# Data-carrying holds on GpSimd, meant to make weight loads and chunk loads take turns

## The chip, the cores and the metric

One NeuronCore of a Trainium2 chip runs the whole program; the other cores are idle. The metric is the device time of one execution in microseconds (us), lower is better. Most executions of the kernel before lie within 1.5% of its fastest; a run that is over 1.5% above the fastest of its kernel is called slow and left out of the ratios. A ratio is the mean time of one kernel's fast runs over the mean of the other's fast runs of the same rounds on the same chip, so it is not quite the ratio of the medians that are quoted beside it. Intervals are 95%.

The engines are TensorE (PE, its weight loads PEld), VectorE (DVE), ScalarE (ACT), GpSimd (POOL) and SyncE (SP). SyncE issues the loads of the inputs and the stores. GpSimd issues the loads of the weights, which are cast to bf16 on the way (6.3 MB of fp32 in HBM; its queue moved 3.15 MB by the page of before).

## The reference

A gated linear attention with a state per head, then an MLP with a squared ReLU, on 3072 tokens (4 batches of 768):

```python
for t in range(S):                       # B, H, S, D = 4, 8, 768, 48
    state = alpha[:, :, t, :, None] * state + einsum('bhd,bhe->bhde', k[:, :, t], v[:, :, t])
    y[:, :, t] = einsum('bhd,bhde->bhe', q[:, :, t], state)
x = y.transpose(0, 2, 1, 3).reshape(B * S, H * D)      # 3072 x 384
h = x @ w_in                                           # w_in 384 x 2048
r = maximum(h, 0); out = (r * r) @ w_out               # w_out 2048 x 384
```

## The kernel before

The tokens come in 24 chunks of 128. A chunk needs four loads of 192 KB: `at` (alpha), `qt`, `kt`, `vt`. Its chain opens on ScalarE with the logarithm of `at`, then TensorE sums the logarithms with a triangular matrix (the matmul that the profile shows as L_s, utri_b), ScalarE takes exponentials, VectorE scales q and k, TensorE does the attention. The MLP runs in groups of chunks: the first group is chunks 0 to 3 with 512 tokens, then single chunks 4 and 5, then pairs.

The kernel doesn't write its instructions in the order in which it emits them. It first fills a `Plan` with operations, each with an engine, an estimated duration and what it depends on. A small list scheduler runs the plan and sorts the operations by planned start. Only then does each `emit`. Calls wrapped in `pin` keep that order on their engine; the compiler may still move those that aren't. The loads of SyncE are not wrapped; in the changed kernel `at` of chunk 4, first of its chunk in the source, is issued eighth, and in e2, which wraps those of chunks 4 and 5, first:

```python
def pin(ins):
    tc.keep_in_program_order(ins)
...
def load_w(dst, src, ready):             # a weight part, on GpSimd
    def e_issue():
        pin(nc.gpsimd.dma_start(out=dst, in_=src))
    issue = add("POOL", W_ISSUE, e_issue, w_gate[0], prio=-3.0, lat=0.0)
    ready.append([add("DMA", WLD, lambda: None, issue, lat=2.0)])
...
def add_gate(d):                         # weights wait for qt of chunk 3
    def e_hold():
        pin(nc.gpsimd.tensor_copy(hold, d["qt"][:, 0, 0:1]))
    w_gate.append(add("POOL", 0.1, e_hold, d["ld_qt"], prio=-6.0))
...
def add_loads(s):                        # the four loads of a chunk, on SyncE
    ...
        def ld(nm=nm, src=src):
            d[nm] = loads.tile([P, H, D], FP32, name=nm)
            nc.sync.dma_start(out=d[nm], in_=src[b, c])
        prev = C[s - LB]["use_" + nm] if s >= LB else None
        d["ld_" + nm] = add("DMA", LD, ld, prev, lat=2.0, at=0.6)
...
DMA_ORDER = [0, 1, 2, 3, "i", "i", "i", "i", "o", "o", "o", 4, "o", 5]
```

`DMA_ORDER` is what the plan believes of the transfers: chunks 0 to 3, four parts of w_in ("i"), w_out in four parts ("o") with chunk 4 before the last. On the chip SyncE and GpSimd issue on their own, so the list does not order the transfers of one against those of the other: `at` of chunk 4, behind seven weight parts in the list, was issued at 15.18 us, the first weight part at 17.52. It does decide when the plan thinks that a chunk is there, and with it where TensorE's fixed order takes the chunk up.

Of the kernel before, what the change touches and what calls it, by code (L numbers as in the profile page):

```python
# [8 lines left out]
FP32 = mybir.dt.float32  # L9
# [101 lines left out]
def kernel(  # L111
# [10 lines left out]
    nc = tc.nc  # L122
    B, H, S, D = q.shape
    HD = H * D
    P = 128
# [6 lines left out]
    FT = d_ff // P  # L132
# [11 lines left out]
    loads = ctx.enter_context(tc.tile_pool(name="loads", bufs=LB))  # L144
# [26 lines left out]
    w_out_b = consts.tile([P, FT, d_model], BF16)  # L171
# [12 lines left out]
    def pin(ins):  # L184
        tc.keep_in_program_order(ins)
# [20 lines left out]
    LD = 1.02  # L206
# [3 lines left out]
    def add(eng, dur, emit, *deps, **kw):  # L210
        return plan.add(Op(eng, dur, emit, deps, **kw))


    w_in_ready, w_out_ready = [], []
    NWP = 4

    W_ISSUE = 0.8
    W_GATE = 3
    hold = consts.tile([P, 1], FP32)

    def load_w(dst, src, ready):
# [5 lines left out]
    def load_w_in(i):  # L227
        w = d_ff // NWP
        sl = slice(i * w, (i + 1) * w)
        load_w(w_in_b[:, :, sl], w_in_r[:, :, sl], w_in_ready)  # L230

    def load_w_out(i):
        w = FT // NWP
        sl = slice(i * w, (i + 1) * w)
        load_w(w_out_b[:, sl, :], w_out_r[:, sl, :], w_out_ready)

    w_gate = []

    def add_gate(d):
        def e_hold():  # L240
            pin(nc.gpsimd.tensor_copy(hold, d["qt"][:, 0, 0:1]))
        w_gate.append(add("POOL", 0.1, e_hold, d["ld_qt"], prio=-6.0))

    C = [dict() for _ in range(NT)]
    state = {}

    def add_loads(s):
        d = C[s]
        b, c = divmod(s, NCH)
        for nm, src in srcs:  # L250
            def ld(nm=nm, src=src):
                d[nm] = loads.tile([P, H, D], FP32, name=nm)
                nc.sync.dma_start(out=d[nm], in_=src[b, c])
            prev = C[s - LB]["use_" + nm] if s >= LB else None
            d["ld_" + nm] = add("DMA", LD, ld, prev, lat=2.0, at=0.6)

    def add_chunk(s):
        d = C[s]
# [219 lines left out]
        add("OUT", 0.55, e_out, ev, at=0.0).late = OUT_LATE  # L478
        return op

    DMA_ORDER = [0, 1, 2, 3, "i", "i", "i", "i", "o", "o", "o", 4, "o", 5]
    for d in DMA_ORDER + [s for s in range(NT) if s not in DMA_ORDER]:
        if d == "i":
            load_w_in(len(w_in_ready))
        elif d == "o":
            load_w_out(len(w_out_ready))
        else:
            add_loads(d)
            add_chunk(d)
            if d == W_GATE:  # L490
                add_gate(C[d])
    b1 = b2 = None
    FIRST_PARTS = [[0, 1], [2, 3]]
    for g in range(NG):
# [74 lines left out]
```

## Time and profile before

| kernel before | |
|---|---|
| time, median of 3 runs | 200.13 us (200.09 to 201.14) |
| span of the profiled execution | 199.3 us |
| TensorE busy | 93% |
| TensorE's one long wait after 24 us | 1.82 us, for part 1 of w_out |
| TensorE idle from 45 to 80 us | 4.4 us |

The page, TensorE's timeline and SyncE's queue are shown in the prediction below. What is not shown there is GpSimd's timeline. Its columns are start, duration, engine and line, operation, output and input, count, and in brackets the idle time before it with what ended it:

```profile
17.40 0.19 POOL L241 COPY hold<-qt 128x1 f32<-128x1 f32 x1 [2.55 <-DMA qt<-in_q_dram]
17.52 2.43 POOL L223 DMA_DIRECT2D w_in_b<-in_moe_w_in_dram  x3
...
21.18 3.01 POOL L223 DMA_DIRECT2D w_out_b<-in_moe_w_out_dram  x4
```

One copy of one column, the gate, keeps all eight weight parts back until qt of chunk 3 has landed, at 17.34 us. Then they are issued together, from 17.52 to 24.19. From there the weights of GpSimd and chunks 4 and 5 of SyncE share the DMA engines: from 30 to 35 us each of the two queues moved 956 packets, 0.73 MB of weights and 0.18 MB of chunks.

The matmul that opens chunk 4 stands late in TensorE's order, after 44 of the 64 w_out matmuls of the first group:

```profile
44.65 0.32 PE L188 MATMUL bank<-L_s,utri_b 128*128 128x384 bf16 x1
```

### The profile page before, as it was taken

Reading aid. Unit: us, or ns where it says so; the run is one execution under the profiler, and the core shown is the slowest. Engines: PE = TensorE matmul, PEld = TensorE weight load, DVE = VectorE, ACT = ScalarE, POOL = GpSimd, SP = SyncE. Lnnn points to the kernel's source line nnn. Section 1 sums busy time; section 2 is a strip of 40 time slices with the busy share of each in tenths; the row PEclk is TensorE's granted clock in tenths of the full one; section 3 lists DMA queues with packets and bytes.
Section 4 is the critical chain, followed back from the end, with each engine's and each line's share of the span. In section 5 each row is a group of like instructions: output and inputs, shape, how many; then the busy total and the mean of one; then the engine's idle time right before and its main releaser. Section 6 shows DMA issues by size and latency. Waiting matters only on the chain.

```text
span 199.3 us, 5184 instructions
## 1 busy us (share of the span) xinstructions
PE 184.8 (93%) x1921; PEld 130.6 (66%) x1924; DVE 138.4 (69%) x359; ACT 132.7 (67%) x380; POOL 23.3 (12%) x46
## 2 busy tenths in 40 slices
PE   7887799699588999999999999999999999999993
PEld 2445444356476787778777777777777777777761
DVE  0599646206999998698888888888888778754300
ACT  3366279317598898668779778867977786656510
POOL 5125801002111111101101101110110000000000
PEclk9999999999999999999999999999999999999999
DMA  6998999999999899989997975231001101100122
GB/s 128 216 194 163 185 191 185 185 187 215 195 216 238 184 190 219 207 174 232 204 233 156 230 171 118 44 79 44 31 9 44 39 3 39 43 26 16 42 81 79
DMA packets 107034, 27.08 MB, mean 136 GB/s; under 512 B 100352, under 2 KB 107008, under 8 KB 107008
## 3 DMA queue, kind: packets, MB, share of 16 engines
q1 hardware_dynamic: 103296, 23.60, 56.4%
q0 software_dynamic: 3712, 3.15, 9.8%
q8 instruction: 15, 0.25, 0.5%
q14 instruction: 11, 0.09, 0.1%
HBM read 25.17 MB, written 4.72 MB: 150 GB/s over the span
## 4 chain that ended last, share of the span: by engine, by line
PE 64%; DVE 2%; DMA 2%; ACT 1%; issue 0%; ACTq 0%; DVEq 0%
PE bank L188 56%; PE bank L191 5%; PE sc L188 2%; DMA out_dram<-ob 2%; PE st L188 1%; DVE gT L441 1%; ACT r L435 1%; DVE sm L342 1%; DVE qkT L326 0%; DVE xT_big L397 0%; ACT ob L472 0%; DVE st L363 0%; ACT L_s L267 0%; ACTq L435 0%; ACTq L472 0%
## 5 line engine op out<-in xcount | busy, mean ns | idle before, releaser
L435 ACT ACTIVATE r<-bank 128x256 bf16<-128x256 f32 (+2 forms) x192 | 68.8, 385 | 23.3 <-PE bank L188 20.2
L188 PE MATMUL bank<-xT_big,w_in_b 128*128 128x256 bf16 (+2 forms) x576 | 79.4, 272 | 1.5 <-ACT r L435 1.0
L188 PE MATMUL bank<-w_out_b,gT 128*128 128x384 bf16 x384 | 74.3, 326 | 1.8 <-DMA w_out_b<-in_moe_w_out_dram 1.8
L441 DVE TENSOR_TENSOR gT<-r 128x256 bf16<-128x256 bf16 (+2 forms) x192 | 55.1, 305 | 19.1 <-ACT r L435 17.6
L188 PEld LDWEIGHTS <-w_in_b 128*128 128x128 bf16 x576 | 48.6, 97 | 16.2 <-issue 2.8
L188 PEld LDWEIGHTS <-gT 128*128 128x128 bf16 x384 | 36.6, 98 | 19.4 <-issue 2.3
L342 DVE TENSOR_TENSOR sm<-sc,utri_b 128x512 bf16<-128x512 f32 x48 | 32.6, 685 | 3.9 <-PE sc L188 3.8
L273 POOL CAST vb<-vt 128x384 bf16<-128x384 f32 x24 | 14.3, 594 | 121.6 <-PE bank L188 68.3
L309 DVE TENSOR_TENSOR qA_s<-qt,A 128x384 bf16<-128x384 f32 x24 | 13.8, 576 | 17.7 <-ACT A L290 17.6
L472 ACT COPY ob<-bank 128x384 f32<-128x384 f32 x23 | 11.0, 480 | 17.7 <-PE bank L188 16.7
L326 DVE COPY qkT<-bank 128x1024 bf16<-128x1024 bf16 x24 | 16.5, 689 | 6.4 <-PE bank L191 6.4
L188 PEld LDWEIGHTS <-qkT 64*128 64x128 bf16 (+1 forms) x272 | 10.8, 95 | 10.4 <-DVE gT L441 4.1
L290 ACT ACTIVATE A<-bank 128x384 bf16<-128x384 f32 x24 | 11.8, 491 | 8.7 <-PE bank L188 8.6
L368 ACT CAST sb<-st 128x384 bf16<-128x384 f32 x20 | 9.6, 479 | 7.5 <-DVE st L363 7.4
L267 ACT ACTIVATE L_s<-at 128x384 bf16<-128x384 f32 x24 | 12.6, 524 | 2.2 <-DMA at<-in_alpha_dram 2.2
L312 DVE TENSOR_TENSOR kI_s<-kt,Ainv 128x384 bf16<-128x384 f32 x24 | 13.8, 576 | 0.2 <-ACT Ainv L294 0.2
L386 ACT CAST xn<-bank 128x384 bf16<-128x384 f32 x24 | 11.5, 478 | 3.1 <-PE bank L188 3.1
L188 PE MATMUL bank<-warm 128*128 128x512 bf16 x33 | 11.2, 477 | 1.3 <-DVE ae_s L181 1.3
L294 ACT ACTIVATE Ainv<-bank 128x384 bf16<-128x384 f32 x24 | 11.8, 492 | 0.0
L188 PE MATMUL sc<-qkT 64*128 64x128 bf16 x192 | 9.5, 218 | 2.1 <-DVE qkT L326 2.0
L363 DVE TENSOR_TENSOR st<-st,ae_s 128x384 f32<-128x384 f32 x20 | 11.1, 556 | 0.0
L191 PE MATMUL bank<-ident_bf,qA_s 128*128 128x128 bf16 x96 | 9.3, 219 | 1.1 <-DVE qA_s L309 0.6
(38 smaller groups left out, 125.9 us busy)
## 6 DMA issues: line engine op xcount, KB each, us to landing
at<-in_alpha_dram SPq DMA_DIRECT2D x24, 192.0 KB, 3.7
qt<-in_q_dram SPq DMA_DIRECT2D x24, 192.0 KB, 3.9
kt<-in_k_dram SPq DMA_DIRECT2D x24, 192.0 KB, 3.8
vt<-in_v_dram SPq DMA_DIRECT2D x24, 192.0 KB, 3.8
out_dram<-ob SPq DMA_DIRECT2D x24, 192.0 KB, 2.3
w_in_b<-in_moe_w_in_dram POOLq DMA_DIRECT2D x4, 384.0 KB, 9.0
w_out_b<-in_moe_w_out_dram POOLq DMA_DIRECT2D x4, 384.0 KB, 16.9
```

What stands on the lines that cost most here:

```text
L188: pin(nc.tensor.matmul(*a, **kw))
L191: pin(nc.tensor.transpose(*a))
L267: pin(nc.scalar.activation(L[:, :, 0:D], d["at"], AF.Ln))
L273: pin(nc.gpsimd.tensor_copy(d["vb"], d["vt"]))
L290: pin(nc.scalar.activation(d["A"], d["pm"][:, 0:HD].rearrange("p (h d) -> p h d", h=H), AF.Exp))
L294: pin(nc.scalar.activation(d["Ai"], d["pm"][:, 0:HD].rearrange("p (h d) -> p h d", h=H), AF.Exp, scale=-1.0))
L309: pin(nc.vector.tensor_mul(qA[:, :, 0:D], d["qt"], d["A"]))
L312: pin(nc.vector.tensor_mul(kI[:, :, 0:D], d["kt"], d["Ai"]))
L326: pin(nc.vector.tensor_copy(d["qkT"], d["pT"]))
L342: pin(nc.vector.tensor_mul(d["sm"][:, hh], d["sc"][:, hh], utri_b.to_broadcast([P, NP, P])))
L435: pin(nc.scalar.activation(box["r"][:, 0:n], box["ph"][:, 0:n], AF.Relu))
L441: pin(nc.vector.tensor_mul(gT[g][:, f, 0:n], box["r"][:, 0:n], box["r"][:, 0:n]))
```

## The change

The intent is that transfers take turns: w_in and the first part of w_out run alone, then chunk 4 is let go, then the second half of w_out, then chunk 5. A load is held by letting GpSimd write one column of its destination tile from a weight part. The load overwrites that column, so it has to wait for the copy, and the copy waits for the weight part (in the changed kernel part 0 landed at 32.73 us, the copy ran from 32.78 to 32.97, the load was issued at 35.51; in e2 the copy ran at 31.10 and the load was issued at 31.32). A second gate holds parts 2 and 3 of w_out behind qt of chunk 4. The core of the diff:

```diff
-    def add_gate(d):
+    def hold_w(d):
         def e_hold():
             pin(nc.gpsimd.tensor_copy(hold, d["qt"][:, 0, 0:1]))
-        w_gate.append(add("POOL", 0.1, e_hold, d["ld_qt"], prio=-6.0))
+        w_gate[:] = [add("POOL", 0.1, e_hold, d["ld_qt"], prio=-6.0)]
+
+    def hold_x(d, i):
+        j = i * FT // NWP
+
+        def e_hold():
+            d["at"] = loads.tile([P, H, D], FP32, name="at")
+            pin(nc.gpsimd.tensor_copy(d["at"][:, 0, 0:1], w_out_b[:, j, 0:1]))
+        d["go"] = add("POOL", 0.1, e_hold, w_out_ready[i][0], prio=-6.0)
 ... (in add_loads)
-                d[nm] = loads.tile([P, H, D], FP32, name=nm)
+                if nm not in d:
+                    d[nm] = loads.tile([P, H, D], FP32, name=nm)
                 nc.sync.dma_start(out=d[nm], in_=src[b, c])
-            d["ld_" + nm] = add("DMA", LD, ld, prev, lat=2.0, at=0.6)
+            d["ld_" + nm] = add("DMA", LD, ld, prev, d.get("go") if nm == "at" else None, lat=2.0, at=0.6)
 ...
-    DMA_ORDER = [0, 1, 2, 3, "i", "i", "i", "i", "o", "o", "o", 4, "o", 5]
+    DMA_ORDER = [0, 1, 2, 3, "i", "i", "i", "i", "o", "o", 4, "o", "o", 5]
+    HOLD_W = (3, 4)
+    HOLD_X = {4: 0, 5: 2}
 ...
+            if d in HOLD_X:
+                hold_x(C[d], HOLD_X[d])
             add_loads(d)
             add_chunk(d)
-            if d == W_GATE:
-                add_gate(C[d])
+            if d in HOLD_W:
+                hold_w(C[d])
```

More of the change, by code (lines that the diff above doesn't have):

```diff
@@ L217 @@
     W_ISSUE = 0.8
-    W_GATE = 3
     hold = consts.tile([P, 1], FP32)
```

## The prediction

> **What bounds the kernel now.** I read the page of the profile first, then the timelines of TensorE (PE), GpSimd (POOL) and SyncE's DMA queue (SP), then the waits and the transfers in windows. The page:
>
> ```profile
> span 199.3 us, 5184 instructions
> PE 184.8 (93%) x1921; PEld 130.6 (66%) x1924; DVE 138.4 (69%) x359; ACT 132.7 (67%) x380; POOL 23.3 (12%) x46
> ...
> PE   7887799699588999999999999999999999999993
> DVE  0599646206999998698888888888888778754300
> ...
> DMA  6998999999999899989997975231001101100122
> ```
>
> TensorE is the bound: 93% busy, nine tenths or more from slice 14 (about 65 us) to the last but one. Its weak slices are among the first thirteen, where the DMA row is mostly at nine. So a load can only cost time in the first 60 us, and every microsecond that TensorE stands there comes out at the end, unless it removes a later wait. The timeline of TensorE says where it stands late in that stretch (start, duration, what, and in brackets the idle time before it and its releaser):
>
> ```profile
> 24.89 10.52 PE L188 MATMUL bank<-xT_big,w_in_b 128*128 128x512 bf16 x48 [0.23 <-DVE xT_big L397]
> 35.28 0.81 PE L188 MATMUL bank<-w_out_b,gT 128*128 128x384 bf16 x4
> 37.90 6.83 PE L188 MATMUL bank<-w_out_b,gT 128*128 128x384 bf16 x40 [1.82 <-DMA w_out_b<-in_moe_w_out_dram]
> ```
>
> The 48 matmuls of the first MLP group run from 24.89 to 35.28, 0.2165 us each; then TensorE waits 1.82 us for the second part of w_out. That wait is what the change is after. Between 45 and 80 us another 4.4 us of TensorE is idle (busy 4.88, 2.81 and 4.31 in the three stretches of 5 us, then 18.64 of 20), mostly on VectorE's and ScalarE's chain of new chunks. The weight parts are late because chunks 4 and 5 are being loaded at the same time. The queue of SyncE in that stretch (start, time that the issue took):
>
> ```profile
> 15.18 1.81 SPq L253 DMA_DIRECT2D at<-in_alpha_dram  x1
> 17.03 0.78 SPq L253 DMA_DIRECT2D qt<-in_q_dram  x1
> ...
> 20.14 4.14 SPq L253 DMA_DIRECT2D at<-in_alpha_dram  x1
> 24.33 5.56 SPq L253 DMA_DIRECT2D qt<-in_q_dram  x1
> 29.93 5.14 SPq L253 DMA_DIRECT2D kt<-in_k_dram  x1
> 35.12 4.25 SPq L253 DMA_DIRECT2D vt<-in_v_dram  x1
> ```
>
> Chunk 4 is the four issues from 15.18, chunk 5 the four from 20.14. [...] Adding each time to landing to its start: chunk 4 lands at 19.3, 23.4, 28.1 and 33.9 us (at, qt, kt, vt), chunk 5 at 39.1, 42.6, 43.9 and 44.7. The parts of w_out land at 35.3, 37.9, 40.6 and 43.2.
>
> [...] transfers from 30 to 35 us (packets, MB):
>
> ```profile
> q0 software_dynamic: 956, 0.73, 92.4%
> q1 hardware_dynamic: 956, 0.18, 33.1%
> ```
>
> GpSimd's weights and SyncE's chunks move one packet each; chunks get 0.18 MB in 5 us, against some 1 MB in 5 us when alone (215 GB/s from 45 to 50 us). [...] the first nine filler matmuls of 512 columns take 4.02 us, 0.45 each, against 0.2165 later, and the 1.82 us wait, [...] is followed by full speed (40 in 6.83 us).
>
> **The change part by part.** I also compared the built instruction orders of the two kernels, and the prediction rests on that.
>
> Added: one more 128x1 GpSimd copy that gates w_out parts 2 and 3 on qt of chunk 4, and two that write one element of the `at` tile of chunks 4 and 5 from w_out parts 0 and 2. The existing one takes 0.19 us; three are 0.6 us on an engine that is 12% busy. Nothing.
>
> Moved, as intended: chunk 4's loads start when w_out part 0 is there. Moved, as built: only the load of `at` depends on the copy. qt, kt and vt of the chunk have no hold, and the loads of SyncE are not pinned in program order. In the built queue, after the sixteen loads of chunks 0-3, stand qt4, kt4, vt4, qt5, kt5, vt5, qt6, and only then at4, then kt6, at5, at6. **So the rivals of the weights are not held: six of the eight loads of chunks 4 and 5 (and qt6) go out at once, while the one that opens the chunk's chain, at4, falls from the first place to the eighth.**
>
> Weights: the first six parts meet the same one-to-one company, so w_out part 0 should land near 35.3 and part 1 near 37.9, as before. Only then are parts 2 and 3 issued (35.7 to 37.3 with a 0.8 us issue each), 13 us later than before. First bytes come about 2.5 us after an issue (17.52 to about 20 for the first), and a part takes 2.65 us in company, so they land at about 42.3 and 44.9.
>
> at4: [...] Before, the eighth transfer after chunk 3 landed at 44.7, after nearly all the weights. The same bytes stand before at4 now, and the DMA engines never rest, so at4 lands at about 44.7 too; the gap in the weights between 36 and 38 us lets the chunks run ahead, so it may be 1 to 2 us earlier, and late last weights could add 1.
>
> TensorE: its built order has the first matmul of chunk 4 (L_s, utri_b) after 45 of the 48 matmuls of the first group (before, it stood after 44 w_out matmuls). It needs ScalarE's Ln of at4, which in ScalarE's order stands ahead of three Relus. So TensorE runs to 24.89 + 45 x 0.2165 = 34.6 and stops. It goes on at 44.7 + 0.1 + 0.53 (Ln) + 0.1 = 45.4: **a stall of 10.8 us**, where before there was a wait of 1.82.
>
> From there. Before, TensorE went from 34.6 to 196.0, 161.3 us, of which 1.8 + 4.4 idle: 155.1 of work. Idle time now: the fill of the chunk pipeline around 50 to 55 us (2.2 us before) is covered, as 64 w_out matmuls (10.4 us) are still to do; the one-chunk groups, where VectorE and ScalarE are at 5.00 and 4.79 of 5 us, still cost some. I take 2.5. Cold clock after the stall: [...] 2 lost. End of TensorE: 45.4 + 155.1 + 2.5 + 2 = 205.0. Last eviction and store as before, 3.3: span 208.3. The time was 0.8 above the span: **209.1 us**. As a difference: +10.8 stall, -1.8 old wait, -1.9 later idle time, +2 clock = +9.1.
>
> **Rivals.** (a) The intent comes true: weights run alone, w_out part 1 is there at about 34 to 35 us, the 1.82 us wait goes and little else: 198 to 199 us. For it: the one-to-one sharing is real. Against it: the queue's order, in which the competing loads are not held. It would also need at4 early. (b) The wait only moves to parts 2 and 3, gated on GpSimd behind part 0: landing at 42.3 and 44.9 where TensorE, without a stall on chunk 4, would need them from about 41 to 42: 3 us in place of 1.8, 201 to 202 us. For it: the chain of hold, issue and first bytes of 6.6 us. Against it: TensorE reaches chunk 4's matmul first, so this is hidden by the larger stall. (c) The stall is real but mostly given back, because afterwards all loads lie far ahead: some 204 us. For it: 4.4 us of idle time to be had. Against it: the work after the stall is 155 us of TensorE and cannot shrink; at most 1.8 + 4.4 us come back.
>
> **Range and chances.** Landing of at4 between 42.5 and 46: -2.2 to +1.3. Idle time after it, 0.5 to 4.5: -2 to +2. Clock, 0 to 2.5: -2 to +0.5. Not all fall together: 205.5 to 212.5. Faster by 2% means under 196.1, less than removing every early idle microsecond could plausibly give: 0.01. Within 2% (196.1 to 204.1) needs (a), (b) or all of (c): 0.07. Slower: 0.92.
>
> **What would show it.** In SyncE's queue, qt4 first after chunk 3 and at4 eighth; at4's time of landing near 44.7. In the waits, TensorE (or the Ln on ScalarE) waiting 9 to 11 us for the load of at from 34.6 on, and no 1.82 us wait for w_out. w_out part 0 landing near 35.3, parts 2 and 3 after 42. Matmuls after the stall at twice their duration for 3 to 5 us. From about 65 us the same dense TensorE row, shifted. Wrong would be: at4 landing before 40 us (the queue passes chunks faster than I think in the gap), TensorE finding other work ahead of chunk 4, or idle time after 45 us above 5 us.

## The result

The changed kernel took 209.59 us (median of 4 runs, 207.20 to 210.32, the last called slow) against 200.19 before. The ratio of the fast runs is 1.042, interval 1.033 to 1.052: slower by 4.2%. The changed kernel's runs spread by 1.5% without a gap, so the rule leaves out no separate state here but the top of the spread; by the medians of all runs it is 4.7%. The profiled execution is the fastest of the four, with a span of 205.5 us.

The page of the changed kernel, the lines that answer to those of before:

```profile
span 205.5 us, 5192 instructions
PE 185.1 (90%) x1920; PEld 130.8 (64%) x1924; DVE 137.8 (67%) x360; ACT 131.1 (64%) x379; POOL 25.9 (13%) x49
...
PE   7878797049999999789999999999999999999993
...
PEclk9999999559999999999999999999999999999999
DMA  6999999999999897999976852240011011101122
```

TensorE's busy time is the same within 0.3 us; of the 6.2 us that the span grew, 5.9 are TensorE standing. (A slower clock makes matmuls longer and so counts as busy: twelve w_out matmuls took 2.87 us at 45.26, where the clock was at 0.50 for the first 1.5 us, against 2.11 in the kernel before. It doesn't show in the sum, as the filler matmuls at the start happened to take 0.7 us less in this execution.) There is a hole at slice 8, from about 36 to 41 us, with slices at either side of it partly empty, and the DMA row is at nine right through it. In the row PEclk two digits are 5: TensorE's clock was halved there (0.50 from 36.5 to 46.8 us).

TensorE's timeline (columns as above):

```profile
24.55 9.87 PE L188 MATMUL bank<-xT_big,w_in_b 128*128 128x512 bf16 x45 [0.23 <-DVE xT_big L405]
43.60 0.48 PE L188 MATMUL bank<-L_s,utri_b 128*128 128x384 bf16 x1 [9.17 <-ACT L_s L275]
...
45.26 2.87 PE L188 MATMUL bank<-w_out_b,gT 128*128 128x384 bf16 x12
```

After 45 of the 48 matmuls of the first group TensorE stands 9.17 us for ScalarE's logarithm of chunk 4. What ScalarE stood for is in the list of waits (from 30 to 48 us; who waited for whom, total, times, longest):

```profile
ACT L_s L275 <- DMA at<-in_alpha_dram: 9.3, 1, 9.3
```

And why the load of `at` came so late stands in SyncE's queue, from the first load after chunk 3 on:

```profile
14.90 1.29 SPq L261 DMA_DIRECT2D qt<-in_q_dram  x1
16.23 0.95 SPq L261 DMA_DIRECT2D kt<-in_k_dram  x1
17.23 0.63 SPq L261 DMA_DIRECT2D vt<-in_v_dram  x1
17.90 3.40 SPq L261 DMA_DIRECT2D qt<-in_q_dram  x1
21.34 4.24 SPq L261 DMA_DIRECT2D kt<-in_k_dram  x1
25.63 5.09 SPq L261 DMA_DIRECT2D vt<-in_v_dram  x1
30.84 4.58 SPq L261 DMA_DIRECT2D qt<-in_q_dram  x1
35.51 0.77 SPq L261 DMA_DIRECT2D at<-in_alpha_dram  x1
```

The held load is the eighth. Six unheld loads of chunks 4 and 5, and one of chunk 6, went ahead and competed with the weights as before. `at` landed 7.43 us after its issue, at 42.9 us. GpSimd shows when the hold let go:

```profile
32.78 0.19 POOL L248 CAST at<-w_out_b 128x1 f32<-128x1 bf16 x1 [11.70 <-DMA w_out_b<-in_moe_w_out_dram]
...
33.32 1.48 POOL L222 DMA_DIRECT2D w_out_b<-in_moe_w_out_dram  x2 [0.22 <-issue]
```

The hold was over at 33.0 us, 10 us before `at` landed. So the time seems to have gone into the place of the load in the queue, not into the hold. Whether that is so, and what each part is worth, is for the experiments.

### The profile page after: what moved, and what is told of

It reads as the page before. It is cut to its first block, busy times and chain, and to the rows that moved or that the text cites. A ratio compares the mean times of both kernels' runs of the same rounds, so it can differ in the third digit from the quotient of the medians.

```text
span 205.5 us, 5192 instructions
## 1 busy us (share of the span) xinstructions
PE 185.1 (90%) x1920; PEld 130.8 (64%) x1924; DVE 137.8 (67%) x360; ACT 131.1 (64%) x379; POOL 25.9 (13%) x49
## 4 chain that ended last, share of the span: by engine, by line
PE 81%; DVE 7%; ACT 4%; DMA 4%; issue 2%; SPq 1%; ACTq 0%
PE bank L188 69%; PE bank L191 7%; DMA at<-in_alpha_dram 4%; PE sc L188 3%; DVE sm L350 2%; PE st L188 1%; DVE kI_s L320 1%; ACT r L443 1%; DVE qA_s L317 1%; DVE st L371 1%; DVE xT_big L405 1%; ACT A L298 1%; ACT L_s L275 1%; DVE qkT L334 1%; SPq L261 1%
## 5 line engine op out<-in xcount | busy, mean ns | idle before, releaser
L188 PE MATMUL bank<-w_out_b,gT 128*128 128x384 bf16 x384 | 75.4, 328 | 0.0
L281 POOL CAST vb<-vt 128x384 bf16<-128x384 f32 x24 | 16.5, 686 | 110.6 <-PE bank L188 81.5
L480 ACT COPY ob<-bank 128x384 f32<-128x384 f32 x22 | 10.5, 478 | 11.0 <-PE bank L188 10.1
L188 PE MATMUL bank<-L_s,utri_b 128*128 128x384 bf16 x24 | 8.2, 343 | 9.4 <-ACT L_s L275 9.4
L188 PEld LDWEIGHTS <-L_s 128*128 128x128 bf16 x96 | 6.1, 99 | 12.7 <-issue 10.5
L188 PE MATMUL bank<-warm 128*128 128x512 bf16 x33 | 10.5, 451 | 1.3 <-DVE ae_s L181 1.3
```

What stands on the lines that cost most here:

```text
L188: pin(nc.tensor.matmul(*a, **kw))
L281: pin(nc.gpsimd.tensor_copy(d["vb"], d["vt"]))
```

## The experiments

The theory, T: the compiler, free to order SyncE's loads, puts those that wait for nothing ahead of the one that is held; `at` of chunk 4 loses its place. TensorE and ScalarE have a fixed order that counts on it, and stand. The rivals: R1, the hold on w_out is itself too late; R2, the second gate costs; R3, TensorE's new order costs by itself. Twelve runs were made in three calls of four; each call ran on one chip with runs of the kernel before beside them, and all outputs were correct.

| run | what differs from the changed kernel | median us | ratio to before | interval |
|---|---|---|---|---|
| e1_after_again | nothing | 209.44 | 1.042 | 1.035 to 1.048 |
| e2_pin_queue | loads of chunks 4, 5 kept in program order | 197.73 | 0.990 | 0.986 to 0.994 |
| e3_plan_late | the plan is told that `at` of chunk 4 is late | 201.20 | 1.009 | 1.007 to 1.012 |
| e4_keep_warm | fillers in the stall, misplaced | 218.54 | 1.094 | 1.089 to 1.100 |
| e5_keep_warm_bank | fillers in the stall | 206.66 | 1.039 | 1.034 to 1.044 |
| e6_after_third | nothing | 209.21 | 1.048 | 1.044 to 1.053 |
| e7_no_hold_x | no holds on chunks | 197.66 | 0.991 | 0.987 to 0.994 |
| e8_hold_on_w_in | as e2, chunk 4 held on w_in part 3 | 197.71 | 0.993 | 0.989 to 0.996 |
| e9_list_only | no holds, no second gate | 195.38 | 0.978 | 0.974 to 0.983 |
| e10_list_earlier | as e9, chunk 4 earlier in the list | 195.86 | 0.980 | 0.974 to 0.985 |
| e11_hold_all | all four loads of the chunks held | 197.79 | 0.992 | 0.989 to 0.995 |
| e12_one_gate | no second gate | 207.44 | 1.041 | 1.037 to 1.045 |

### e1 and e6: the changed kernel again

> The changed kernel unaltered, once more, so that the others are compared with it on one chip. Theory T (the unheld q, k, v loads overtake the held alpha load of chunk 4 in SyncE's queue, and TensorE and ScalarE stand in their fixed order for it): 207 to 211 us, a stall of 9 to 11 us ahead of chunk 4's first matmul, and the differences between executions are differences in when at of chunk 4 lands. Any rival: the same total time.

> The changed kernel unaltered, for comparison on the same chip with the three others: 207 to 211 us, at of chunk 4 landing at 43 to 45 us.

Both came out as expected. In the three profiles of this kernel the stall was 9.17, 11.06 and 9.66 us. The one with the longest stall had `at` land last: chunk 4's first matmul ran at 43.60, 44.73 and 44.34 us. Of e1's six runs three count as slow, since one was as fast as 207.06; nothing here rests on them.

### e2: the queue's order alone

```diff
-                nc.sync.dma_start(out=d[nm], in_=src[b, c])
+                ins = nc.sync.dma_start(out=d[nm], in_=src[b, c])
+                if s in (4, 5):
+                    pin(ins)
```

> Holds, gates and the orders of TensorE, ScalarE and VectorE around chunk 4 as in the changed kernel; only the loads of chunks 4 and 5 are kept in program order on SyncE, so that at of chunk 4 is first and q, k, v stand behind it. T: w_out part 0 lands at 30 to 32.5 us (weights alone), at of chunk 4 at 34 to 36, the stall falls from 9-11 us to 0.5-2, no cold clock, a wait of about 0.5 us for w_out part 3; 196 to 199 us, a little faster than before. Rival R1 (the hold on w_out part 0 is itself too late, whatever the queue's order): stall 6 us or more, 204 us or more. Rival R2 (the second gate, w_out parts 2 and 3 behind qt of chunk 4, costs): waits of 3 us or more for w_out between 40 and 46 us, 200 to 203 us.

197.73 us, 11.7 us under the changed kernel's median in the same call and 1.0% under the kernel before. The holds, the gates and TensorE's order up to chunk 5 are those of the changed kernel. SyncE's queue of the run, the last load of chunk 3 and the first three of chunk 4, and TensorE at the opening of chunk 4:

```profile
13.94 0.96 SPq L261 DMA_DIRECT2D vt<-in_v_dram  x1
31.32 0.37 SPq L261 DMA_DIRECT2D at<-in_alpha_dram  x1
31.73 0.58 SPq L261 DMA_DIRECT2D qt<-in_q_dram  x1
32.35 1.57 SPq L261 DMA_DIRECT2D kt<-in_k_dram  x1
```

```profile
35.51 0.32 PE L188 MATMUL bank<-L_s,utri_b 128*128 128x384 bf16 x1 [0.85 <-ACT L_s L277]
```

Now the hold really keeps the queue empty for 16 us, w_out part 0 lands at 31.1, and the stall falls from about 10 us to 0.85. R1 expected 6 us or more of it; it falls. R2 expected waits for w_out of 3 us or more; there was none in this profile.

### e3: the plan knows that `at` is late

```diff
-            ... d.get("go") if nm == "at" else None, lat=2.0, at=0.6)
+            ... d.get("go") if nm == "at" else None, lat=12.0 if nm == "at" and s == 4 else 2.0, at=0.6)
```

> The queue as wrong as in the changed kernel (same 24 first loads), but the planner is told that at of chunk 4 comes 10 us later, so TensorE's order has chunk 4's first matmul after 48 of the 64 w_out matmuls, about as before. T says that it takes both, the late load and an order that relies on an early one: stall for at gone; w_out part 3 lands at 42 to 45 us and makes TensorE wait 1 to 3.5 us in its place; 200.5 to 204 us. If the order of the queue alone were the cause: still 207 or more. If the fixed order alone: 199 to 200.5, as before.

201.20 us. The queue is as in the changed kernel, seven loads ahead of `at`, but TensorE's order has other work at that point. Its two waits are now for weights:

```profile
36.44 5.36 PE L188 MATMUL bank<-w_out_b,gT 128*128 128x384 bf16 x32 [0.97 <-DMA w_out_b<-in_moe_w_out_dram]
42.67 2.11 PE L188 MATMUL bank<-w_out_b,gT 128*128 128x384 bf16 x12 [0.88 <-DMA w_out_b<-in_moe_w_out_dram]
```

So the same late load costs 0.9% where the order doesn't count on it and 4.2% where it does. Neither half is enough: with the right queue the early order is good (e2), with the late order the wrong queue is nearly harmless (e3). The wait for part 3 was expected at 1 to 3.5 us and came out a little under, at 0.88. R3 alone is ruled out by e2, which has the early order and is fast.

### e4 and e5: what the halved clock costs

```diff
         def e_p0():
+            if s == 4:
+                wp = banks[4].tile([P, 512], FP32, name="bank4")
+                for _ in range(40):
+                    mm(wp, lhsT=warm[:, 0:P], rhs=warm, start=True, stop=True)
```

> The changed kernel with 40 filler matmuls of 512 columns (40 x 0.2165 = 8.7 us) ahead of chunk 4's first matmul on TensorE, where it stands idle anyway. It tells the cold clock's part of the loss apart: T with the clock term as predicted: granted clock stays at 1.0, the first w_out matmuls after the stall take their usual 0.165 us each in place of 0.24, and the time is 1.5 to 2 us below the unaltered kernel of the same call. If the clock cost nothing: the same time within 0.5 us.

e4 was a mistake in the experiment, and 218.54 us its result, 9.1 us above e1. The fillers wrote a PSUM bank whose last value a Relu still had to read, and that Relu stood on ScalarE behind the blocked logarithm (TensorE waited 10.63 us for it). They ran after the stall, from 45.0 to 56.2 us, so it says nothing of the clock. e5 writes them to the bank that the next matmul overwrites:

```diff
             pm = d["pm"] = psum(p0, [P, 512], FP32)
+            for _ in range(44 if s == 4 else 0):
+                mm(pm, lhsT=warm[:, 0:P], rhs=warm, start=True, stop=True)
             mm(pm[:, 0:HD], lhsT=utri_b[:, 0, :], rhs=L[:, :, 0:D], start=True, stop=True)
```

> The filler experiment again, mended. In the one before, the fillers wrote a PSUM bank that a Relu behind the blocked Ln still had to read, so they ran after the stall (45.0 to 56.2 us) and not in it. Here 44 fillers (9.5 us) write the bank that chunk 4's first matmul takes next anyway, which is free. They should run from about 34 to 43.5 us. With the clock term as predicted: granted clock 1.0, the 12 w_out matmuls after the stall in 2.1 us in place of 2.9 to 3.1, and 1.5 to 2.2 us below the unaltered changed kernel of the same call, so 207 to 208 us. If the clock costs nothing at the end: equal within 0.5 us.

TensorE's timeline of e5, and below it of e6 for comparison:

```profile
33.98 9.66 PE L188 MATMUL bank<-warm 128*128 128x512 bf16 x44
44.63 0.32 PE L188 MATMUL bank<-L_s,utri_b 128*128 128x384 bf16 x1 [0.99 <-ACT L_s L276]
...
45.54 2.11 PE L188 MATMUL bank<-w_out_b,gT 128*128 128x384 bf16 x12
```

```profile
44.34 0.48 PE L188 MATMUL bank<-L_s,utri_b 128*128 128x384 bf16 x1 [9.66 <-ACT L_s L275]
...
46.00 3.13 PE L188 MATMUL bank<-w_out_b,gT 128*128 128x384 bf16 x12
```

The fillers keep the clock at 1.00, and twelve w_out matmuls take 2.11 us in place of 3.13. The mean of the fast runs is 207.07 against 209.11 for e6 on the same chip: the clock is worth 2.0 us of the loss, give or take 1.4 (95%, worked out from the six runs of each). e6's profile agrees: its clock stayed halved for 3.7 us after TensorE went on, which would cost 1.9. The stall remains, as it must.

### e7: no holds at all

```diff
-    HOLD_X = {4: 0, 5: 2}
+    HOLD_X = {}
```

> The new transfer list, the second gate (w_out parts 2 and 3 behind qt of chunk 4) and the new order of TensorE, but no holds on chunk loads: SyncE's queue is in program order and chunk 4 competes with the weights as before. Theory T: no stall at chunk 4 (at lands at about 19 us), w_out part 1 late as before (36 to 38 us) with a wait of 0.5 to 1.6 us at TensorE's fifth w_out matmul; 197.5 to 199.5 us. If the second gate costs (R2): a wait for w_out part 2 or 3 of over 1 us and 200 us or more. If the gain of the pinned queue over before comes from the holds and the weights landing sooner, this kernel should be 1 us or more slower than 197.7; if it comes from TensorE's new order, which takes chunk 4 up earlier, it should be equal within 0.7 us.

197.66 us, a ratio of 0.991 where e2 has 0.990. The chunks compete with the weights as before the change, and the only wait for a weight was 0.75 us, for part 1. So the holds, even where they work, buy nothing that this kernel doesn't have without them. What e2 gained over the kernel before did not come from weights that land sooner. What was left was the plan's order, the second gate, or both.

### e8: the hold one weight part earlier

```diff
-            pin(nc.gpsimd.tensor_copy(d["at"][:, 0, 0:1], w_out_b[:, j, 0:1]))
+            pin(nc.gpsimd.tensor_copy(d["at"][:, 0, 0:1], w_in_b[:, 0, f0:f0 + 1] if s4 else w_out_b[...]))
```

> The pinned queue, with the hold of chunk 4 on the last part of w_in in place of the first of w_out, one weight part earlier (some 2.2 us). The pinned kernel still stood 0.85 us for at of chunk 4. T: at lands at about 32 to 33 us, no stall there, w_out part 1 about 1 us later but still there before its use at 36.5 to 37, parts 2 and 3 about 2 us earlier; 196.3 to 197.5 us. If sharing delays w_out part 1 past its use: a wait of up to 1 us in its place and 197.5 to 198.3.

197.71 us, ratio 0.993: no better than e2. The copy ran at 29.00 in place of 31.10 us, but qt of chunk 4 landed at about 35.2 against 35.6: the load of `at` took 5.2 us from issue to landing in place of 3.5, while w_out parts 0 and 1 were under way. That sharing ate the two microseconds is the likely reading. The stall was 0.57 in place of 0.85 us. The expectation for `at` (32 to 33 us) was too early.

### e9 and e10: the list alone

```diff
-    HOLD_W = (3, 4)
-    HOLD_X = {4: 0, 5: 2}
+    HOLD_W = (3,)
+    HOLD_X = {}
```

> Only the planner's transfer list of the change (chunk 4 ahead of the second half of w_out): no holds on chunk loads, no second gate, so the real queues of SyncE and GpSimd issue what they issue before the change, in the same order. It tells the list (TensorE's order) apart from gates and holds. If the planner's order alone makes the gain of e2 and e7: 197 to 198.5 us, a wait of 0.5 to 1.5 us for w_out part 1, no idle time of over 1.5 us between 50 and 55 us. If the second gate made it: 199 to 200.5, as before.

195.38 us (194.46 to 195.47), 2.2% under the kernel before (1.7 to 2.6): the fastest of all with e10, and faster than expected. The built queues of SyncE and GpSimd issue the chunks and weights of this stretch in the order of before the change. The only difference that is left is a list that tells the plan that chunk 4 comes before the third part of w_out. TensorE:

```profile
34.20 0.33 PE L188 MATMUL bank<-L_s,utri_b 128*128 128x384 bf16 x1
...
37.05 1.46 PE L188 MATMUL bank<-w_out_b,gT 128*128 128x384 bf16 x8 [1.12 <-DMA w_out_b<-in_moe_w_out_dram]
```

Chunk 4 is taken up at 34.20 in place of 44.65 us and waits for nothing, as its `at` has been there since about 19. The wait for w_out is still 1.12 us. The larger gain is behind it. From 45 to 60 us TensorE was busy 12.00 us before and 13.95 here, from 60 to 80 us 18.64 and 19.68: of 4.4 us of idle time 1.4 are left. While chunk 4's chain fills, TensorE has w_out matmuls to do.

e7 and e9 differ in the second gate alone. The windows from 60 to 80 us of e7, then of e9 (length, then busy time of PE, PEld, DVE, ACT and POOL, granted clock, DMA share, GB/s):

```profile
60.00:80.00 20.00, 18.27 (x229) 13.68 (x227) 17.16 (x42) 15.14 (x46) 2.33 (x5) 1.00 1.04 229
```

```profile
60.00:80.00 20.00, 19.68 (x249) 15.18 (x247) 18.00 (x50) 16.43 (x52) 2.06 (x4) 1.00 0.99 213
```

e7 stands 1.4 us longer there, although no wait for a gated part shows. On the chip the gate held nothing back. In e7's GpSimd timeline it runs without a wait, and parts 2 and 3 of w_out landed at 38.7 and 41.5 us, in e9 at 39.7 and 42.4:

```profile
21.73 0.21 POOL L240 COPY hold<-qt 128x1 f32<-128x1 f32 x1
```

What is left is what the gate tells the plan (no run told the plan of the gate without putting it on the chip): with it the later groups run in another order, and a row of waits of 0.2 to 0.4 us on ScalarE appears at 72 to 78 us. e2, e8 and e11 show the same waits, and so does the changed kernel, at 82 to 89 us; e9 and e12, without the gate, do not. The means of the fast runs of e7 and e9 are 197.63 and 195.11, 2.5 us apart in two calls whose runs of before differ by 0.1 us in the mean. The two profiled executions are only 1.2 us apart; e7's was the fastest of its six.

In e10 the list is moved one place further:

```diff
-    DMA_ORDER = [0, 1, 2, 3, "i", "i", "i", "i", "o", "o", 4, "o", "o", 5]
+    DMA_ORDER = [0, 1, 2, 3, "i", "i", "i", "i", "o", 4, "o", "o", "o", 5]
```

> As the list alone, with chunk 4 one weight part earlier in the planner's list (after the first part of w_out). The real queues stay the same; TensorE takes chunk 4's first matmul after 36 of the 48 matmuls of the first group (31.7 us), its at is there at 19.3 us, kt at 28, vt at 34. Expected if taking chunk 4 up earlier still pays: 196.5 to 197.5 us. If ScalarE, which is at 4.6 of 5 us there, only pushes its Relus later: 197.5 to 198.5, equal to the list alone.

195.86 us, under both expected ranges; two of its six runs were slow (199.4 and 201.3), the others lie on e9's. Whether taking chunk 4 up nine matmuls earlier still pays is not settled; it doesn't show.

### e11 and e12: the holds done fully, and without the gate

```diff
-            d["at"] = loads.tile([P, H, D], FP32, name="at")
-            pin(nc.gpsimd.tensor_copy(d["at"][:, 0, 0:1], w_out_b[:, j, 0:1]))
+            for nm, _ in srcs:
+                d[nm] = loads.tile([P, H, D], FP32, name=nm)
+                pin(nc.gpsimd.tensor_copy(d[nm][:, 0, 0:1], w_out_b[:, j, 0:1]))
 ...
-            ... d.get("go") if nm == "at" else None, ...
+            ... d.get("go"), ...
```

> The change carried out as its words say: the hold on w_out parts 0 and 2 is written into all four tiles of chunks 4 and 5, so that q, k and v are held as well (eight GpSimd copies in place of two), both gates kept. SyncE's built queue then has at of chunk 4 first. T (the missing holds are the cause): no stall of over 2 us at chunk 4; 197 to 199 us, as the pinned queue. Rival R1 (data-carrying holds cost in themselves): 203 us or more.

197.79 us, 0.992. This is the change as its words have it. It works as intended: `at` is first in the queue again, TensorE doesn't stand for it, and R1 in the form given here falls. TensorE's wait for weights is 0.64 us, for part 3. It is no faster than e7, which holds nothing. The queue is in order with all four loads held and with none held (e7): it is the hold on `at` alone that turned it.

e12 is the changed kernel without the second gate:

```diff
-    HOLD_W = (3, 4)
+    HOLD_W = (3,)
```

> The changed kernel without its second gate: at of chunks 4 and 5 still held on w_out parts 0 and 2, all eight weight parts issued together. In SyncE's built queue at of chunk 4 is now ninth after chunk 3 (qt, kt of chunk 6 ahead of it). T: the loads ahead share with all weights without the gap, so at lands 0 to 1 us later than in the changed kernel, at 44 to 46 us, stall 10 to 12 us, 208.5 to 211.5 us. If the second gate makes part of the loss (R2): 1 us or more faster than the changed kernel, under 208.3.

207.44 us. T expected a later `at` and got it: the stall was 11.21 us, chunk 4's first matmul ran at 45.48. But its time, 208.5 to 211.5 us, was missed, and R2's mark of 208.3 was met. With 1.041 against 1.042 and 1.048 the times alone leave the gate's share of the loss between nothing and 1.5 us. The profiles say more. e1 has nearly the same stall, 11.06 us, and a span of 206.9 us against 205.3. The windows from 80 to 100 us of e1, then of e12 (columns as for e7):

```profile
80.00:100.00 20.00, 18.23 (x227) 14.52 (x226) 16.75 (x47) 15.79 (x50) 2.32 (x4) 1.00 0.91 187
80.00:100.00 20.00, 19.91 (x237) 15.63 (x233) 17.96 (x50) 16.68 (x52) 4.55 (x4) 1.00 0.92 191
```

From 60 to 100 us TensorE stood 2.5 us in e1 and 1.3 in e12. So with the second gate the changed kernel loses about what e7 loses by it, 1.1 to 1.6 us here, beside the stall of 11 us.

## Why the prediction was right

**The bound and the order.** The prediction rested on the built order of the queue and of TensorE. Both ran as read: `at` was the eighth load after chunk 3, and TensorE stopped after 45 matmuls, at 34.4 us (34.6 predicted).

**The stall.** Predicted 10.8 us with `at` at 44.7; measured 9.17, 11.06 and 9.66 us with `at` at 42.9 in the first. The text allowed 1 to 2 us earlier for the gap in the weights; that size came, but not for that reason. In the eleven profiles whose chunk loads compete with the weights, with the second gate or without, the eighth load after chunk 3 landed 26.3 to 27.7 us after GpSimd issued the first weight (27.2 in the kernel before, 27.0 in the changed one). In both profiles, before and changed, all 120 transfers of SyncE and all eight of GpSimd landed in the order of their issue. The same bytes took the same time, as the prediction says first; the gap moved nothing, and `at` was early because the weights began 1.6 us earlier. e2, which changes only the queue, and e3, which changes only the order, show that it takes both.

**The weights.** Part 0 landed at 32.7 us, not 35.3, and part 2 at 39.1, not 42.3. The gate on qt of chunk 3 opened at 15.8 in this execution and at 17.4 in the profile of before; it opened at 15.6 to 17.4 us in the twelve profiles of the experiments, whatever the kernel. The first packet of the weights moved 2.2 us after the first issue before (19.71 after 17.52) and 1.7 us after it here (17.63 after 15.93). I took one execution's gate for a fixed time. It mattered: the end was set by `at`, and the landing of `at` moves with the gate.

**The clock.** Predicted 2 us; e5 against e6 measured 2.0. That a stall of 10 us would halve the clock, and for how long, no run had shown before: in the profile of before the longest wait after 24 us is 1.82 us, with the clock at 1.00 after it. The nine slow fillers at its start, 4.02 us against 9 x 0.2165 = 1.95, come to the same size, but the trace records no clock before 7.3 us. From the profile: the granted clock was 0.50 from 43.60, when TensorE went on, to 46.8 us, 3.2 us at half speed, which would be 1.6; in e1 and e6 it was 3.7.

**The idle time later.** Predicted 2.5 us after the stall; in the windows from 47 to 100 us TensorE was idle 2.5 (0.69 from 60 to 80, 1.76 from 80 to 100). The fill at 50 to 55 us was covered, as said. The size is right, the reason only in part: the prediction put it on the one-chunk groups, and e12 has 1.3 of it without the second gate, so about half comes with the second gate, which the prediction did not reckon with.

**The sum.** For the two profiled executions: 9.2 (stall) + 1.6 (clock) - 1.8 (old wait) - 1.9 (4.4 less 2.5 of later idle time) - 0.3 (the first group began earlier) = 6.8, against 6.2 measured; durations of matmuls are modelled in the records. The median, 2.4 us above the profiled execution, would fit a longer stall such as e1's; that wasn't traced. One reading was wrong: the time was taken as 0.8 us above the span, by setting the median of other executions beside the span of the profiled one. That execution took 200.97 us, and in every run of the result the time is 1.7 us above its own span. The predicted span, 208.3, lies above the middle of the four (205.5, 207.3, 208.4 and 208.6), so the two errors partly cancel. That the forecast of 209.1 is 0.5 us from the median is partly luck; the mechanism is not.

**The rivals.** (a), the intent come true, was given 198 to 199 us; e11 is that kernel, at 197.8. The order behind it was better than I assumed, but the transfers were not the reason. (b), a wait that moves to parts 2 and 3, shows at 0.64 us in e11 and 0.88 in e3, at most a third of the 3 us given. (c), that most comes back later, is refuted by the result.

What the prediction did not see is that the good part of the change was the list, one line: 2.2% by itself (1.7 to 2.6). I weighed the list only as the place where TensorE would stand.

## What to carry to other kernels

A hold has to sit on every load that it is meant to hold, or the queue has to be pinned: where the compiler may reorder, a load that waits can be overtaken by those that don't, here by seven, and end behind its own chunk. Look at the built order of the queue before believing the source. And separate what an edit does on the chip from what it tells a planner: here the planner's new order was worth 2.2%, the second gate, which held nothing back in e7, took 1.3% of it back, so most likely through the plan, the holds done fully added nothing, and the holds done by half turned it into a loss of 4%.

## What else the traces show of the queues and the clock

- In the changed kernel too the two queues moved nearly the same number of packets, 943 and 944 from 28 to 33 us, but unequal ones: 0.73 MB of weights against 0.18 MB of chunks in that time.
- In the changed kernel a load of 192 KB took 0.4 to 1.3 us to issue up to 17.9 us, and 3.4 to 5.1 us from 17.90 to 35.4 us. From the fourth load on, three or four earlier loads were unfinished at the start of issues of both kinds; the difference is that the loads ahead landed 4.0 to 6.4 us apart from 18.8 to 35.1 us, and 0.6 to 1.6 us apart before that. The issues went at about the pace of the landings: they began 3.4 to 5.2 us apart.
- In the changed kernel the clock halved at 36.5 us, about 2.1 us after the last matmul, and came back 3.2 us after TensorE went on. In e1, e4, e6 and e12 it halved 4.5, 2.1, 3.1 and 4.5 us after the last matmul. So 2.1 us of standing was enough in two of these five profiles, and the 1.82 us in the kernel before was not.
- In e3 the clock halved at 53.8 us and stayed so for 3.4 us, after four microseconds in which no single wait was above 0.79 us but TensorE was busy less than half the time from 50 to 52 (0.69 of 2 us) and mostly with small attention matmuls and transposes. The window line of e3 (columns as above) shows the halved clock with TensorE busy:

```profile
54.00:55.00 1.00, 0.99 (x13) 0.68 (x13) 1.00 (x3) 0.46 (x2) 0.15 (x1) 0.50 1.01 202
```
